# High and low halves in tiles of their own, the shared tap first and on head 1, and a new spread of first loads, weight conversion and softmax products

## The chip, the cores and the metric

The kernel runs on one core of a Trainium2 chip. The metric is the device time of one execution in microseconds, the median of the runs. The core's engines work side by side, each through its own list in order: PE (the matrix engine, its weight loads shown as PEld), DVE (the vector engine), ACT (the scalar engine), POOL, and SP, which issues DMAs. Engines wait for one another through semaphores.

## The reference

```
qn = q / (norm(q, axis=1) + 1e-6);  kn = k / (norm(k, axis=1) + 1e-6)      # B=4, N=6336, C=256
s = kn^T @ qn / tau                     # 256 x 256 per batch: attention between channels
a = softmax(s);  x = v @ a              # the attention's output
g = sum over k of conv_w[k] * x[t-4+k]  # causal convolution along N, five taps per channel
out = (sigmoid(g) * (x @ w_val)) @ w_out
```

q, k, v and the output are float32, 4 x 6336 x 256. The weights come as 64-bit floats; the kernel takes them as pairs of 32-bit words and turns them into float32 on the chip.

## The kernel before, in words

**Row groups.** For each batch b, q and k are read in 17 groups of three row tiles (128 rows each); group 0 has one full tile and one of 64 rows. `group_tasks` loads a group into `raw`; ACT squares it (`sq`), and DVE or POOL adds the squares into running sums (`acc_ps` on DVE, `acc` on POOL). PE multiplies k by q into the batch's 256 x 256 sum in PSUM (`s_ps`, L481). A tile is multiplied either whole in fp32 (operands `raw`) or split: ACT casts it to a high half (L413), POOL subtracts to get the low half (L416), and PE multiplies high by high, low by high and high by low. High and low lie in one tile, `hi`. Of batch 0, the first groups are whole and then two tiles of three.

**Softmax.** Once all groups of a batch are in, a chain of small tasks `("M", b, ...)` makes the attention matrix. DVE joins the sums of squares (acc, L518); PE sums over rows (norms, L514); ACT takes the root (L525); DVE inverts (L529 to L534); ACT makes a diagonal (L539); PE spreads it (L546); DVE scales (L550); ACT takes the exponentials (L556) and divides (L568); PE transposes (L581) and multiplies by `w_val` (combine, L591). High and low halves of both results (L572, L575 on POOL; high_w L595 on ACT, low_w L598 on DVE) are what the steps multiply by.

**Steps.** 52 steps n, 13 a batch, cover 508 rows each (240 the last of a batch). A step loads v, transposes it (DVE, L659), casts it high (ACT, L663) and low (POOL, L666). For each head h, a half of the 256 channels, PE makes x (X, `x_ps`, L674), ACT multiplies by tap 0 into `gate` (G, L697) and DVE adds the other taps (D, L700). ACT takes the sigmoid (Z, L711), PE makes the values (U, `val_ps`), DVE multiplies (B, L718), ACT and POOL make high and low halves (H, L724; J, L727), and PE makes the output (F, L746), which ACT copies (L755) and SP stores. In the late steps (36 to 50), which have no row groups beside them, the last tap of one head is shared: ACT makes it in a tile of its own, `part` (G+, L705), and POOL adds it (D+, L708).

**Weights.** `prepare_weights` (L309 to L337) is a generator of DVE operations on 32-bit words, one task each. `w_ps` is its scratch in PSUM, `w_raw` the words in SBUF; val and out are 128 x 512, the convolution's weight is 128 x 10.

**What sets the order.** Nothing is ordered by hand but PE's list, `line`, built at the end: all groups of batch 0, then steps with groups of later batches between them, and the four softmax products of a batch dropped in one at a time by `chain`. The class `Plan` holds tasks with costs, dependencies and buffers, works out due times from `line`, and picks for each engine in turn; `emit` fixes that order in the program. Costs of tasks are numbers in the source. `WANTED` gives due times in us for the weights' tasks.

Of the kernel before, what the change touches and what calls it, by code (L numbers as in the profile page):

```python
# [17 lines left out]
P = 128  # L18
GROUP = 3
# [8 lines left out]
class Plan:  # L28
# [65 lines left out]
    def run(self, line):  # L94
# [21 lines left out]
        dma_free, lanes = 0.0, []  # L116
# [18 lines left out]
        while len(order) < len(T):  # L135
# [76 lines left out]
def kernel(  # L212
# [70 lines left out]
    w_raw = {}  # L283
# [22 lines left out]
    def prepare_weights(part):  # L306
# [6 lines left out]
        if WORDS == 2:  # L313
# [15 lines left out]
            nc.vector.tensor_scalar(up, up, 0xFFE00, 3, ALU.bitwise_and, ALU.logical_shift_left)  # L329
            yield  # L330
            nc.vector.tensor_tensor(up, up, f, ALU.bitwise_or)
# [10 lines left out]
    PREP = {"val": 10, "conv": 10, "out": 9}  # L342

    def weight_tasks():
# [5 lines left out]
        for part in ("val", "conv", "out"):  # L350
            gen = {}
            n = PREP[part] if WORDS == 2 else 1
            for k in range(n):
# [4 lines left out]
                if part != "conv" and k == 6:  # L358
                    cost = 1.25
# [4 lines left out]
                  "out": lambda: WORDS == 2 and nc.scalar.copy(wo_hi.rearrange("p h e -> p (h e)"), w_raw["out"][:, :, 1].bitcast(F32))}[part],  # L364
                 deps=[("prep", part, n - 1)], uses=[holds[part]])
# [7 lines left out]
    def group_tasks(b, g):  # L373
# [14 lines left out]
        def load():  # L388
            raw = t["raw4"] = raw_p.tile([P, 2, GROUP, C], F32, name="raw")
            for s, src in ((0, q), (1, k)):  # L390
                eng = nc.scalar if b == 0 and g < 2 and s else nc.sync
                main = src[b, 0:RP * P].rearrange("(p j) c -> p j c", j=RP)
                eng.dma_start(out=raw[:, s, 0:n, :], in_=main[:, j0_:j0_ + n, :])
                if g == 0 and REST:
                    eng.dma_start(out=raw[0:REST, s, n, :], in_=src[b, RP * P:N])
            if (b, g) == (0, 1):
# [3 lines left out]
        issues = (4 if g == 0 and REST else 2) // (2 if b == 0 and g < 2 else 1)  # L400
# [6 lines left out]
        for u, (np_, ja, jb) in enumerate(split):  # L407
            r, js = slice(0, np_), slice(ja, jb)

            def cast(r=r, js=js, u=u):  # L410
                if u == 0:
                    t["hi"] = split_p.tile([P, GROUP, 2, 2, C], F32R, name="hi")
                nc.scalar.copy(t["hi"][r, js, :, 0, :], t["raw"][r, js, :, :])  # L413

            def low(r=r, js=js):
                nc.gpsimd.tensor_tensor(t["hi"][r, js, :, 1, :], t["raw"][r, js, :, :], t["hi"][r, js, :, 0, :].bitcast(F32), ALU.subtract)  # L416
# [35 lines left out]
        for u, part in enumerate(squares):  # L452
# [3 lines left out]
            for j in range(ja, jb):  # L456
                task(("A", b, g, j), dict(DVE=0.6, POOL=1.25), None, lambda engine, np_=np_, j=j: add(np_, j, engine),
# [14 lines left out]
        def mms(np_, j, whole=True, halves=((0, 0), (0, 1), (1, 0))):  # L472
            r = slice(0, np_)
            stop = g == NG - 1 and (np_, j) == rows[-1] and (whole or len(halves) > 1)
            for h in range(NH):
                if whole:
                    ops = [(dealt(t["raw"][r, j, 1, :], h), t["raw"][r, j, 0, :])]
                else:
                    ops = [(dealt(t["hi"][r, j, 1, x, :], h), t["hi"][r, j, 0, y, :]) for x, y in halves]
                for n_, (lhs, rhs) in enumerate(ops):  # L480
                    nc.tensor.matmul(st["s"][:, h, :], lhs, rhs, start=False, stop=stop and h == NH - 1 and n_ == len(ops) - 1)  # L481
            if (b, g) == (0, 0) and j == n:
# [21 lines left out]
    def softmax_tasks(b):  # L504
# [410 lines left out]
```

## Time and profile before

| | us |
|---|---|
| median of 3 runs | 604.43 (603.49 to 607.92) |
| profiled execution, its own time | 606.84 |
| its span in the profile | 605.0 (1.84 lie outside) |
| granted TensorE clock | 1.0 |

Each row of a group gives line, engine, operation, tiles and the count, then busy us and mean ns. Rows in order of time begin with the start in us and the time taken; a bracket gives idle time ahead of it and what ended that. The span starts at 0; batch 0's products end near 51 us, the batches' steps begin near 65, 214, 359 and 504.

### The profile page before, as it was taken

The page shows a single profiled execution, that of the slowest core. Times are in us where ns is not written, and L with a number is a line of the kernel's source. Part 1 is how long each engine was busy: PE and PEld are TensorE (multiplying, and loading weights), DVE is VectorE, ACT ScalarE, POOL GpSimd, SP SyncE. Part 2 cuts the span into 40 slices and gives each one's busy share as a digit, 9 for nine tenths or more (in the row PEclk, how much of TensorE's full clock was granted, in tenths as well). Part 3 has the DMA queues.
Part 4 walks back from the last instruction along what each step waited for, and adds up shares of the span by engine and source line. Part 5 has one row for each costly group of instructions (what it writes and reads, how often), then busy time and mean ns, then how long its engine had stood idle before and what let it go on. Part 6 is the DMA issues. An engine that isn't in the chain of part 4 may idle for free.

```text
span 605.0 us, 10549 instructions
## 1 busy us (share of the span) xinstructions
PE 594.2 (98%) x3659; PEld 533.2 (88%) x3659; DVE 510.2 (84%) x789; ACT 474.3 (78%) x588; POOL 504.1 (83%) x241
## 2 busy tenths in 40 slices
PE   8999999999999999999999999999999999999996
PEld 6988898999989988998998988998988998888886
DVE  2997799999877999969777899978977979888774
ACT  5768999789889979689689978878677876677645
POOL 3977999999979999989986999988973777577653
PEclk9999999999999999999999999999999999999999
DMA  8999958696674968889465888769646353554213
GB/s 297 387 364 282 232 126 200 170 192 141 194 192 126 224 151 219 167 201 204 126 175 140 218 203 198 162 148 233 143 122 132 79 143 91 131 138 112 59 57 121
DMA packets 154944, 105.84 MB, mean 175 GB/s; under 512 B 111114, under 2 KB 137994, under 8 KB 154890
## 3 DMA queue, kind: packets, MB, share of 16 engines
q1 hardware_dynamic: 154387, 104.45, 68.5%
q10 hardware_dynamic: 503, 0.71, 0.4%
q8 instruction: 29, 0.48, 0.3%
q14 instruction: 25, 0.20, 0.1%
HBM read 79.18 MB, written 25.95 MB: 174 GB/s over the span
## 4 chain that ended last, share of the span: by engine, by line
PE 52%; DVE 24%; POOL 7%; issue 6%; ACT 6%; DMA 4%; SPq 1%; POOLq 0%; DVEq 0%; ACTq 0%
PE s_ps L481 13%; PE x_ps L674 13%; DVE gate L700 12%; PE o_ps L746 12%; PE val_ps L674 12%; DVE acc_ps L444 6%; POOL g_lo L727 3%; DVE gate L718 3%; DMA v_raw<-in_v_dram 2%; DMA raw<-in_k_dram 2%; POOL gate L708 1%; DVE v_raw L659 1%; POOL hi L416 1%; ACT g_hi L724 1%; PE o_ps L591 1%
## 5 line engine op out<-in xcount | busy, mean ns | idle before, releaser
L700 DVE SCALAR_TENSOR_TENSOR gate<-x_ps,wa,gate 128x508 f32<-128x508 f32 (+1 forms) x401 | 272.5, 717 | 28.3 <-POOL g_lo L727 9.1
L416 POOL TENSOR_TENSOR hi<-raw,hi 128x1536 fp32r<-128x1536 f32 (+2 forms) x65 | 182.5, 2811 | 16.8 <-ACT hi L413 11.5
L727 POOL TENSOR_TENSOR g_lo<-gate,g_hi 128x1016 fp32r<-128x1016 f32 (+2 forms) x52 | 120.2, 2312 | 20.7 <-ACT g_hi L724 20.7
L444 DVE TENSOR_TENSOR acc_ps<-acc_ps,sq 128x512 f32<-128x512 f32 (+1 forms) x145 | 100.5, 693 | 42.9 <-ACT sq L440 39.2
L666 POOL TENSOR_TENSOR v_lo<-v_raw,v_hi 128x1024 fp32r<-128x1024 f32 (+1 forms) x52 | 123.4, 2373 | 6.6 <-ACT v_hi L663 5.2
L481 PE MATMUL s_ps<-hi 128*128 128x256 f32 x918 | 126.5, 288 | 1.3 <-POOL hi L416 1.3
L481 PEld LDWEIGHTS s_ps<-hi 128*128 128x128 f32 x918 | 117.9, 196 | 4.8 <-POOL hi L416 2.7
L674 PE MATMUL x_ps<-v_hi,w 128*128 128x512 f32 (+2 forms) x416 | 110.3, 385 | 1.5 <-DVE gate L700 1.5
L674 PE MATMUL val_ps<-v_hi,w 128*128 128x508 f32 (+1 forms) x416 | 107.7, 380 | 0.0
L440 ACT ACTIVATE sq<-raw 128x1536 f32<-128x1536 f32 (+2 forms) x68 | 95.9, 1413 | 7.3 <-DVE acc_ps L444 5.3
L674 PEld LDWEIGHTS val_ps<-v_hi,w 128*128 128x128 f32 x416 | 75.9, 188 | 14.9 <-DVE gate L718 0.2
L413 ACT CAST hi<-raw 128x1536 fp32r<-128x1536 f32 (+2 forms) x65 | 77.8, 1200 | 13.1 <-DMA raw<-in_k_dram 13.1
L724 ACT CAST g_hi<-gate 128x1016 fp32r<-128x1016 f32 (+3 forms) x54 | 52.8, 978 | 44.6 <-DVE gate L718 44.3
L674 PEld LDWEIGHTS x_ps<-v_hi,w 128*128 128x128 f32 x416 | 72.7, 188 | 14.6 <-issue 2.3
L746 PE MATMUL o_ps<-wo_hi,g_hi 128*127 128x256 f32 (+1 forms) x396 | 79.2, 281 | 0.0
L746 PE MATMUL o_ps<-wo_lo,g_hi 128*127 128x256 f32 (+1 forms) x396 | 79.0, 281 | 0.0
L755 ACT COPY o_sb<-o_ps 127x512 f32<-127x512 f32 (+1 forms) x99 | 57.5, 589 | 27.4 <-PE o_ps L746 27.2
L444 POOL TENSOR_TENSOR acc<-acc,sq 128x512 f32<-128x512 f32 (+1 forms) x47 | 61.1, 1301 | 14.4 <-ACT sq L440 12.7
L718 DVE TENSOR_TENSOR gate<-val_ps,gate 128x508 f32<-128x508 f32 (+1 forms) x104 | 67.0, 656 | 4.3 <-ACT gate L711 4.3
L697 ACT ACTIVATE gate<-x_ps,wa 128x508 f32<-128x508 f32 (+1 forms) x104 | 68.2, 662 | 1.2 <-PE x_ps L674 1.1
L711 ACT ACTIVATE gate<-gate 128x1016 f32<-128x1016 f32 (+1 forms) x52 | 53.2, 1024 | 18.5 <-DVE gate L700 18.5
L746 PE MATMUL o_ps<-wo_hi,g_lo 128*127 128x256 f32 (+1 forms) x396 | 64.0, 284 | 1.9 <-POOL g_lo L727 1.9
(84 smaller groups left out, 740.7 us busy)
## 6 DMA issues: line engine op xcount, KB each, us to landing
raw<-in_q_dram SPq DMA_DIRECT2D x64, 384.0 KB, 6.2
v_raw<-in_v_dram SPq DMA_DIRECT2D x192, 128.0 KB, 6.0
raw<-in_k_dram SPq DMA_DIRECT2D x63, 384.0 KB, 6.8
out_dram<-o_sb SPq DMA_DIRECT2D x47, 448.0 KB, 3.2
out_dram<-o_sb SPq DMA_DIRECT2D x47, 60.0 KB, 3.0
v_raw<-in_v_dram SPq DMA_DIRECT2D x16, 64.0 KB, 2.1
out_dram<-o_sb SPq DMA_DIRECT2D x3, 240.0 KB, 2.6
raw<-in_q_dram SPq DMA_DIRECT2D x4, 128.0 KB, 3.1
```

Of the source, the lines that this page charges most:

```text
L413: nc.scalar.copy(t["hi"][r, js, :, 0, :], t["raw"][r, js, :, :])
L416: nc.gpsimd.tensor_tensor(t["hi"][r, js, :, 1, :], t["raw"][r, js, :, :], t["hi"][r, js, :, 0, :].bitcast(F32), ALU.subtract)
L440: nc.scalar.activation(t["sq"][0:np_, ja:jb], t["raw"][0:np_, ja:jb], AF.Square)
L444: eng.tensor_tensor(st[key][0:np_], st[key][0:np_], t["sq"][0:np_, j], ALU.add)
L481: nc.tensor.matmul(st["s"][:, h, :], lhs, rhs, start=False, stop=stop and h == NH - 1 and n_ == len(ops) - 1)
L666: nc.gpsimd.tensor_tensor(t["vl"][:, :, 0:g, :], t["v"], t["vh"][:, :, 0:g, :].bitcast(F32), ALU.subtract)
L674: nc.tensor.matmul(dst, weights[b][:, which, ws, ch, hs], vs[:, ch, at + lo:at + hi_], start=n_ == 0, stop=n_ == len(ops) - 1)
L697: nc.scalar.activation(t["gate"][:, h, 0:w], t["x", h][:, 0:w], AF.Copy, scale=cw[:, h, 0:1])
L700: nc.vector.scalar_tensor_tensor(t["gate"][:, h, 0:w], t["x", h][:, k_:k_ + w], cw[:, h, k_:k_ + 1], t["gate"][:, h, 0:w], ALU.mult, ALU.add)
L718: nc.vector.tensor_tensor(t["gate"][:, h, 0:w], t["val", h][:, 0:w], t["gate"][:, h, 0:w], ALU.mult)
L727: eng.tensor_tensor(t["gl"][:, hs, 0:w], t["gate"][:, hs, 0:w], t["gh"][:, hs, 0:w].bitcast(F32), ALU.subtract)
L746: nc.tensor.matmul(t["o", p][0:rows, u * C:(u + 1) * C], gs[:, h, j * rows:(j + 1) * rows], ws[:, h, :], start=(u, n_) == (0, 0) if HEADS ...
```

## The change

1. The split tile `hi` becomes two tiles, `hi` (both operands' high halves) and `lo`. The products are the same.
2. In steps 36 to 50 the shared last tap is that of head 1 instead of head 0, and POOL adds it before DVE's taps of that head instead of after head 0's.
3. First loads: q's 64 rows go to ACT's queue and group 1's k to SP's. The 64-row tile's products follow group 2's. Only group 0's first tile has extra zero products behind it.
4. Loads of `w_val` and `w_out` move ahead of group 6's, those of the convolution's weight behind them.
5. In the weight conversion two operations that wrote to `w_raw` become three that write to PSUM.
6. The softmax products of batches 1 to 3 are spread by `SPREAD`: each of the last three skips one call of `chain`.
7. Costs in the planner change, and it counts table loads of ACT.

```diff
-START, HOP, DRAIN, SLOT, FLIGHT, REACH, RATE = 4.8, 0.12, 0.4, 0.45, 4.5, 1.6, 340000.0
+START, HOP, DRAIN, SLOT, FLIGHT, REACH, RATE = 4.8, 0.12, 0.22, 0.45, 4.5, 1.6, 340000.0
...
-WANTED = {("load", "conv"): 16, ("load", "val"): 17, ("load", "out"): 24, ("ready", "val"): 40, ("ready", "out"): 48}
+SPREAD = (0, 1, 1, 1)
+TABLE = 1.28
+WANTED = {("load", "conv"): 30, ("load", "val"): 17, ("load", "out"): 26, ("ready", "val"): 40, ("ready", "out"): 48}
...
-            nc.vector.tensor_scalar(up, up, 0xFFE00, 3, ALU.bitwise_and, ALU.logical_shift_left)
+            low = wo_lo.rearrange("p h e -> p (h e)") if part == "out" else w
+            nc.vector.scalar_tensor_tensor(low, lo, 2.0 ** -35, fs, ALU.mult, ALU.mult)
             yield
-            nc.vector.tensor_tensor(up, up, f, ALU.bitwise_or)
+            nc.vector.tensor_scalar(f, f, 3, None, ALU.logical_shift_right)
             yield
-            dst = wo_lo.rearrange("p h e -> p (h e)") if part == "out" else fs
-            nc.vector.scalar_tensor_tensor(dst, lo, 2.0 ** -35, fs, ALU.mult, ALU.mult)
+            nc.vector.scalar_tensor_tensor(f, up, 0xFFE00, f, ALU.bitwise_and, ALU.bitwise_or)
+            yield
+            nc.vector.tensor_scalar(f, f, 3, None, ALU.logical_shift_left)
+            w_high[part] = fs
             if part != "out":
                 yield
-                nc.vector.tensor_tensor(w, fs, up.bitcast(F32), ALU.add)
+                nc.vector.tensor_tensor(w, w, fs, ALU.add)
...
-                eng = nc.scalar if b == 0 and g < 2 and s else nc.sync
+                eng = nc.scalar if b == g == 0 and s else nc.sync
...
-                    eng.dma_start(out=raw[0:REST, s, n, :], in_=src[b, RP * P:N])
+                    (nc.scalar if b == 0 else nc.sync).dma_start(out=raw[0:REST, s, n, :], in_=src[b, RP * P:N])
...
-                    t["hi"] = split_p.tile([P, GROUP, 2, 2, C], F32R, name="hi")
-                nc.scalar.copy(t["hi"][r, js, :, 0, :], t["raw"][r, js, :, :])
+                    t["hi"], t["lo"] = [split_p.tile([P, GROUP, 2, C], F32R, name=name) for name in ("hi", "lo")]
+                nc.scalar.copy(t["hi"][r, js], t["raw"][r, js, :, :])
...
-            few = K - 1 if shared and h == 0 else K
+            few = K - 1 if shared and h == 1 else K
+            if few < K:
+                part_i = ("sq", "part", n)
+                task(("G+", n), "ACT", 0.06 + 0.51 * part, lambda h=h: last_tap(h), deps=[("G", n, h)], uses=[x_i, part_i], takes=[part_i])
+                task(("D+", n), "POOL", 0.1 + 1.15 * part, lambda h=h: add_tap(h), deps=[("G+", n)], uses=[part_i, gate_i])
...
-            if few < K:
-                part_i = ("sq", "part", n)
-                task(("G+", n), "ACT", 0.06 + 0.51 * part, lambda h=h: last_tap(h), deps=[("X", n, h)], uses=[x_i, part_i], takes=[part_i])
-                task(("D+", n), "POOL", 0.1 + 1.15 * part, lambda h=h: add_tap(h), deps=[("G+", n), ("D", n, h, few - 1)], uses=[part_i, gate_i])
...
+        if (b, g) == (0, 0):
+            kept.extend(rows[2:])
+            rows = rows[:2]
         line.extend(rows)
+        if (b, g) == (0, 2):
+            line.extend(kept)
         if g == NG - 1:
-            pending.extend(mm(b, "norms", "spread", "transpose", "combine"))
+            names = mm(b, "norms", "spread", "transpose", "combine")
+            for key, wait in zip(names, SPREAD if b else (0,) * 4):
+                pending.extend([None] * wait + [key])
```

Lines of the changed program lie six or so further down. The first place is SP's queue at the start; the 128x256 rows are group 0's full tile, 64x256 its rest, 128x768 a later group. Before:

```order
L393 DMA raw_106<-in_q_dram 128x256
L395 DMA raw_106<-in_q_dram 64x256
L393 DMA raw_111<-in_q_dram 128x768
L393 DMA raw_115<-in_q_dram 128x768
L393 DMA raw_115<-in_k_dram 128x768
```

Now, up to the loads of the two big weights:

```order
L399 DMA raw_106<-in_q_dram 128x256
L399 DMA raw_112<-in_q_dram 128x768
L399 DMA raw_112<-in_k_dram 128x768
L399 DMA raw_115<-in_q_dram 128x768
...
L399 DMA raw_132<-in_q_dram 128x768
L399 DMA raw_132<-in_k_dram 128x768
L308 DMA w_raw_137<-in_moe_w_val_dram 128x2x512
L308 DMA w_raw_152<-in_moe_w_out_dram 128x2x512
L399 DMA raw_175<-in_q_dram 128x768
```

The 64 rows of q left this queue, group 1's k (`raw_112`) came into it, and both weights stand ahead of group 6 (`raw_175`).

The second place is DVE around the end of batch 0's sums of squares (acc_all) up to the invert of the norms. Before:

```order
L331 TENSOR_TENSOR w_raw_230<-w_raw_230,w_ps_353 128x512
L334 SCALAR_TENSOR_TENSOR wo_lo_100<-w_raw_230,w_ps_353 128x512
L444 TENSOR_TENSOR acc_ps_126<-acc_ps_126,sq_461 128x512 x2
L444 TENSOR_TENSOR acc_ps_126<-acc_ps_126,sq_471 128x512 x2
L518 TENSOR_TENSOR acc_all_502<-acc_ps_126,acc_137 128x512
L529 TENSOR_SCALAR o_ps_506<-o_ps_506 128x4
```

Now:

```order
L450 TENSOR_TENSOR acc_ps_128<-acc_ps_128,sq_476 128x512 x2
L326 TENSOR_SCALAR w_ps_424<-w_raw_273 128x10
L328 TENSOR_SCALAR w_ps_424<-w_ps_424 128x10
L524 TENSOR_TENSOR acc_all_508<-acc_ps_128,acc_135 128x512
L330 TENSOR_SCALAR w_ps_424<-w_ps_424 128x10
L332 SCALAR_TENSOR_TENSOR w_ps_424<-w_raw_273,w_ps_424 128x10
...
L345 TENSOR_TENSOR wa_97<-wa_97,w_ps_424 128x10
L369 RECIPROCAL rtau_95<-tau_sb_96 128x1
L665 STREAM_TRANSPOSE v_raw_388<-v_raw_388 128x2x512
L535 TENSOR_SCALAR o_ps_519<-o_ps_519 128x4
```

Two conversions of the convolution's weight stand ahead of the sum, seven more, the reciprocal and the first step's transpose between the sum and the invert.

The third place is ACT in a late step, from its sigmoid (L711, now L717) to the next step's output copies. Before:

```order
L711 ACTIVATE gate_5715<-gate_5715 128x1016
L697 ACTIVATE gate_5803<-x_ps_5784,wa_97 128x508
L705 ACTIVATE part_5805<-x_ps_5784,wa_97 128x508
L697 ACTIVATE gate_5803<-x_ps_5796,wa_97 128x508
```

Now:

```order
L717 ACTIVATE gate_5781<-gate_5781 128x1016
L703 ACTIVATE gate_5870<-x_ps_5850,wa_97 128x508
L703 ACTIVATE gate_5870<-x_ps_5863,wa_97 128x508
L711 ACTIVATE part_5882<-x_ps_5863,wa_97 128x508
```

The part (L705, now L711) went from the place behind head 0's gate to behind head 1's. On POOL, in the same steps, before:

```order
L708 TENSOR_TENSOR gate_5803<-gate_5803,part_5805 128x508
L727 TENSOR_TENSOR g_lo_5869<-gate_5715,g_hi_5868 128x1016
L666 TENSOR_TENSOR v_lo_5848<-v_raw_5648,v_hi_5847 128x1024
L708 TENSOR_TENSOR gate_5892<-gate_5892,part_5894 128x508
```

Now:

```order
L714 TENSOR_TENSOR gate_5870<-gate_5870,part_5882 128x508
L672 TENSOR_TENSOR v_lo_5914<-v_raw_5714,v_hi_5913 128x1024
L733 TENSOR_TENSOR g_lo_5936<-gate_5781,g_hi_5935 128x1016
L714 TENSOR_TENSOR gate_5959<-gate_5959,part_5971 128x508
```

The low half of a later step's v now comes ahead of the gate's low half, right behind the shared tap's add. On DVE, the first of a step's taps no longer waits for the part, and head 1's first tap waits for POOL's add.

More of the change, by code (lines that the diff above doesn't have):

```diff
@@ L33, in __init__, with task @@
         self.tasks = {}
-    def task(self, key, engine, cost, emit, deps=(), uses=(), takes=(), lead=()):
+    def task(self, key, engine, cost, emit, deps=(), uses=(), takes=(), lead=(), table=None):
         assert key not in self.tasks, key
-        self.tasks[key] = dict(key=key, engine=engine, cost=cost, emit=emit, deps=list(deps), lead=dict(lead), uses=list(dict.fromkeys(list(uses) + list(takes))),
+        self.tasks[key] = dict(key=key, engine=engine, cost=cost, emit=emit, deps=list(deps), lead=dict(lead), table=table, uses=list(dict.fromkeys(list(uses) + list(takes))),
                                takes=list(takes), order=len(self.tasks))
@@ L115, in run @@
                 opened(key)
-        dma_free, lanes = 0.0, []
+        dma_free, lanes, table = 0.0, [], None
         order = []
@@ L168, in run @@
                 free[e] = start + self.duration(t, e)
+                if t["table"] and t["table"] != table:
+                    table = t["table"]
+                    free[e] += TABLE
                 end = free[e] + (DRAIN if e == "PE" else HOP if e else 0)
@@ L282 @@
     parts_w = {"val": wa[:, 0:NW], "conv": wa[:, NW:], "out": wb}
-    w_raw = {}
+    w_raw, w_high = {}, {}
     def load_weights(*names):
@@ L357, in weight_tasks @@
                 cost = 0.6 if part != "conv" else 0.1
-                if part != "conv" and k == 6:
-                    cost = 1.25
                 task(("prep", part, k), "DVE", cost, emit, deps=[("load", part) if k == 0 else ("prep", part, k - 1)],
@@ L363, in weight_tasks @@
                  {"val": lambda: None, "conv": lambda: nc.vector.reciprocal(rtau, tau_sb),
-                  "out": lambda: WORDS == 2 and nc.scalar.copy(wo_hi.rearrange("p h e -> p (h e)"), w_raw["out"][:, :, 1].bitcast(F32))}[part],
-                 deps=[("prep", part, n - 1)], uses=[holds[part]])
+                  "out": lambda: WORDS == 2 and nc.scalar.copy(wo_hi.rearrange("p h e -> p (h e)"), w_high["out"])}[part],
+                 deps=[("prep", part, n - 1)], uses=[holds[part], ("bank", "w", part)])
     def dealt(row, h):
@@ L456, in group_tasks @@
             for j in range(ja, jb):
-                task(("A", b, g, j), dict(DVE=0.6, POOL=1.25), None, lambda engine, np_=np_, j=j: add(np_, j, engine),
+                task(("A", b, g, j), dict(DVE=0.7, POOL=1.25), None, lambda engine, np_=np_, j=j: add(np_, j, engine),
                      deps=[("S", b, g, u)] + [("B", b, x) for x in accs], uses=[sq_i] + list(accs.values()))
@@ L478, in mms @@
                 else:
-                    ops = [(dealt(t["hi"][r, j, 1, x, :], h), t["hi"][r, j, 0, y, :]) for x, y in halves]
+                    ops = [(dealt(t[("hi", "lo")[x]][r, j, 1, :], h), t[("hi", "lo")[y]][r, j, 0, :]) for x, y in halves]
                 for n_, (lhs, rhs) in enumerate(ops):
                     nc.tensor.matmul(st["s"][:, h, :], lhs, rhs, start=False, stop=stop and h == NH - 1 and n_ == len(ops) - 1)
-            if (b, g) == (0, 0) and j == n:
+            if (b, g, j) == (0, 0, 0):
                 idle(2)
@@ L837 @@
     todo = [(bg, rows_of[bg]) for bg in all_groups]
-    pending = []
+    pending, kept = [], []
     def take_group():
@@ L850, in chain @@
             if pending:
-                line.append(pending.pop(0))
+                key = pending.pop(0)
+                if key:
+                    line.append(key)
     for _ in range(NG):
@@ L870 @@
             if all_steps[n + 1][0] != all_steps[n][0]:
-                chain(4)
+                chain(len(pending))
             line += [("X", n + 1, h) for h in range(NH)]
```

29 lines of the change are left out of this document (15 added, 14 removed).

## The prediction

> **What bounds the kernel now.** I read the page's share of busy time first, then the chain that ended last, then what PE, the matrix engine, waited for (us in total, times, longest).
>
> ```profile
> PE 594.2 (98%) x3659; PEld 533.2 (88%) x3659; DVE 510.2 (84%) x789; ACT 474.3 (78%) x588; POOL 504.1 (83%) x241
> PE 52%; DVE 24%; POOL 7%; issue 6%; ACT 6%; DMA 4%; SPq 1%; POOLq 0%; DVEq 0%; ACTq 0%
> ...
> PE o_ps L746 <- POOL g_lo L727: 1.9, 3, 0.9
> PE x_ps L674 <- DVE gate L700: 1.5, 2, 0.8
> PE s_ps L481 <- POOL hi L416: 1.3, 3, 0.6
> ```
>
> PE is busy for 98% of 605.0 us, and every product is kept. So the change can win only PE's pauses, its slow first stretch and the small gaps between matmuls. The orders elsewhere change too (square sums dealt anew between DVE and POOL), where PE is full. The second line warns that 24% of the chain is DVE: in places PE is paced by another engine. The other three rows give the pauses: POOL's low halves at the end (1.9 us), vector taps (1.5), POOL's low halves in batch 0 (1.3).
>
> ```profile
> 30.00:45.00 15.00, 14.07 (x80) 12.36 (x79) 14.73 (x23) 9.66 (x10) 10.88 (x9) 1.00 1.01 365
> 180.00:195.00 15.00, 15.00 (x104) 13.96 (x104) 9.81 (x15) 14.99 (x19) 12.43 (x6) 1.00 0.48 141
> 570.00:585.00 15.00, 14.16 (x79) 12.16 (x78) 10.09 (x16) 9.49 (x14) 11.02 (x6) 1.00 0.23 71
> ```
>
> The table by stage has window, then busy us of PE, PEld, DVE, ACT, POOL. In 180 to 195 PE is full, in 30 to 45 and 570 to 585 about 0.9 us is open. The steady middle offers nothing; four places do, and I price each.
>
> **Start.** Two groups of products, from 3.6 to 7.6 and from 11 to 16 us, and three rows in order of time:
>
> ```profile
> L481 PE MATMUL s_ps<-raw 128*128 128x256 f32 (+1 forms) x8 | 4.1, 673 | 0.0
> L481 PE MATMUL s_ps<-raw 128*128 128x256 f32 x25 | 5.6, 379 | 0.0
> ...
> 5.70 1.35 PEld L481 LDWEIGHTS s_ps<-raw 64*128 64x128 f32 x4 [0.65 <-DMA raw<-in_q_dram]
> 8.72 7.95 PE L481 MATMUL s_ps<-raw 128*128 128x256 f32 x32
> 1.18 0.54 ACTq L395 DMA_DIRECT2D raw<-in_k_dram  x1
> ```
>
> Early products take 673 ns instead of 379, and the 64-row tile's run in that slow stretch. The change puts its four products behind group 2 and lets group 1's two loads follow q0 directly. Four of eight took half of 4.1 us; four of the 32 that follow take an eighth of 7.95, 1.0. So PE could be 1.05 earlier, and 0.65 more if the pause for that tile goes; k0 now stands behind one more issue on ACT's queue, 0.54. That is 0 to 1.7 for PE alone. It doesn't count by itself: the norms of batch 0 wait for the sum of squares on DVE, priced next. It counts as cover for PE's other waits up to there.
>
> **Sum of squares in batch 0.** DVE is 14.73 of 15 us busy; its work ahead of the sum sets it.
>
> ```profile
> 27.74 3.19 DVE L329 TENSOR_SCALAR w_raw<-w_raw 128x512 int32<-128x512 int32 x1
> L329 DVE TENSOR_SCALAR w_raw<-w_raw 128x512 int32<-128x512 int32 x2 | 3.6, 1809 | 0.0
> 20.05 0.69 DVE L329 TENSOR_SCALAR w_raw<-w_raw 128x10 int32<-128x10 int32 x1
> L331 DVE TENSOR_TENSOR w_raw<-w_raw,w_ps 128x512 int32<-128x512 int32 x2 | 1.4, 678 | 0.0
> L323 DVE TENSOR_SCALAR w_ps<-w_ps 128x512 int32<-128x512 int32 x2 | 1.4, 700 | 0.0
> 51.03 0.69 DVE L518 TENSOR_TENSOR acc_all<-acc_ps,acc 128x512 f32<-128x512 f32 x1
> 51.78 1.08 PE L514 MATMUL o_ps<-ones,acc_all 128*128 128x1 f32 x8 [0.24 <-DVE acc_all L518]
> ```
>
> Two big weights lose L329 (3.6 us together) and L331 (1.4), 5.0, and gain three operations each in forms of L323 (0.70), 4.2: 0.8 less. The convolution weight's ten operations (nine near 0.17, as the small L529 of the next fence but one, and the 0.69) and the reciprocal come to 2.4; only two of its new ones, 0.3, still stand ahead of the sum: 2.0 less. Together 2.8. Bounds: 0.3 if the long operation's stall (3.19 - 0.69) only moves to a neighbour, 3.1 if loads that start earlier add 0.3. I take 2.5, near the full count, as the new forms read or write PSUM as L323 does, and its two take 0.70 each. So the norms start at 49.3 instead of 51.78. [...]
>
> PE must keep up. Its waits for POOL before that (1.3) shrink, since the two high-high products of a tile no longer stand behind POOL; at 7.95/32 = 0.25 each the pair covers 0.5 us of each wait, and the longest is 0.6. With the earlier start that is enough.
>
> The two big weights now load ahead of group 6, both at once.
>
> ```profile
> 15.00:30.00 15.00, 15.00 (x86) 13.95 (x85) 14.03 (x28) 11.49 (x12) 15.00 (x13) 1.00 1.02 386
> ```
>
> The transfers are full there (share 1.02). At 386 GB/s the 1.05 MB take 2.7 us; the convolution's loads that stood there before leave, so group 6 lands some 2.2 us later, and ACT's squares with it. DVE then has conversions to do, so I price that at nothing; without that cover up to 2.2 us of the 2.5 are gone.
>
> **Chain of batch 0.** What was moved off comes back here.
>
> ```profile
> 53.08 0.17 DVE L529 TENSOR_SCALAR o_ps<-o_ps 128x4 f32<-128x4 f32 x1 [1.36 <-ACT o_ps L525]
> ...
> 57.32 1.24 DVE L659 STREAM_TRANSPOSE v_raw<-v_raw 128x1024 f32<-128x1024 f32 x1
> ...
> 63.75 1.59 PEld L591 LDWEIGHTS o_ps<-wa,at 128*128 128x128 f32 x8 [0.39 <-ACT at L585]
> ```
>
> Between the sum and the invert (L529) now stand seven conversions and the reciprocal, 0.17 each, and the first transpose, 1.24: 2.6 us in a hole of 1.36, so the chain is 1.2 us later behind its sum; at best nothing, as the transpose no longer stands at 57.32, ahead of the exponentials' total. PE has next-batch products to fill, as before, but paused 0.39 before the combine already. Step 0's low_w moves behind its eight taps, but its value products move behind step 1's gate products, which cover it. I give back 1.1, a little less (0 to 1.7, with 0.6 for that if the cover is short). The stage nets 2.5 - 1.1 = **1.4** (-1.4 to 2.5).
>
> **First steps of batches 1 and 2.**
>
> ```profile
> 207.67 2.94 DVE L444 TENSOR_TENSOR acc_ps<-acc_ps,sq 128x512 f32<-128x512 f32 x4
> 210.52 5.83 DVE L700 SCALAR_TENSOR_TENSOR gate<-x_ps,wa,gate 128x508 f32<-128x508 f32 x8
> 215.06 1.15 PE L674 MATMUL x_ps<-v_hi,w 128*128 128x512 f32 x4 [0.77 <-DVE gate L700]
> ```
>
> PE waits 0.77 us for a tap that started late, behind four sums of squares; the waits at both places are 1.5 by the second table. Between the last short taps and these stand five sums now instead of seven, 2 x 0.73 = 1.5 us less, so the waits can go. Bounds 0 and 0.95 each, with the small gaps around; the chain's later pieces land in the same stretch, so I take 0.65 each, **1.3**. Smaller waits of this sort at other places: 0.2 (-0.5 to 0.5).
>
> **Late steps with the shared tap.**
>
> ```profile
> 515.48 0.40 PE L746 MATMUL o_ps<-wo_hi,g_hi 128*127 128x256 f32 x2
> 523.79 0.40 PE L746 MATMUL o_ps<-wo_hi,g_hi 128*127 128x256 f32 x2
> 565.76 0.40 PE L746 MATMUL o_ps<-wo_hi,g_hi 128*127 128x256 f32 x2
> 574.24 0.40 PE L746 MATMUL o_ps<-wo_hi,g_hi 128*127 128x256 f32 x2
> 573.10 1.05 ACT L711 ACTIVATE gate<-gate 128x1016 f32<-128x1016 f32 x1
> 574.06 0.67 ACT L697 ACTIVATE gate<-x_ps,wa 128x508 f32<-128x508 f32 x1
> 574.63 0.68 ACT L705 ACTIVATE part<-x_ps,wa 128x508 f32<-128x508 f32 x1
> 575.39 2.18 DVE L700 SCALAR_TENSOR_TENSOR gate<-x_ps,wa,gate 128x508 f32<-128x508 f32 x3 [2.39 <-ACT part L705]
> 581.61 1.05 ACT L711 ACTIVATE gate<-gate 128x1016 f32<-128x1016 f32 x1
> 571.15 1.28 POOL L708 TENSOR_TENSOR gate<-gate,part 128x508 f32<-128x508 f32 x1 [2.01 <-DVE gate L700]
> 584.64 0.74 PE L746 MATMUL o_ps<-wo_hi,g_lo 128*127 128x256 f32 x4 [0.84 <-POOL g_lo L727]
> ```
>
> A step takes PE 8.31 us at 515, 8.48 at 565. From one sigmoid (L711) to the next is 8.51 us: ACT's sigmoid, gate and shared part, then DVE's taps, which start on the part (the row at 575.39 says so). That loop is longer than PE's 8.31, so a lag builds, paid from 565 on in steps of 8.48 and at 584.64 in a wait for POOL's low half. After the change the first tap waits for the first gate alone, 574.63 - 574.06 = 0.57 earlier: the loop is 7.9, under 8.31, and PE sets the pace. Gain: 1.9 of waits, some four steps of 0.17 and about 0.2 of small gaps around each of the three waits, 3.2; bounds 0.7, if only the stretching goes and the ends stay, and 3.5. I take **3.2**. The added wait is DVE's on POOL: head 1's taps wait for POOL's add (1.28). On ACT the part now comes third, so it ends about 1.1 us after the first tap starts and the add 1.3 later; ahead of head 1's first tap stand four taps at 0.73 and two products of the step before, near 0.7 each (as a tap): 4.3. Slack 1.9 if POOL is free. Behind a waiting tap stand the step's other taps, B and the sigmoid.
>
> **The sum.** 1.4 + 1.3 + 0.2 + 3.2 = 6.1; 0.7 off for waits that new orders bring and no row shows: 5.4. Span 605.0 - 5.4 = 599.6; the profiled execution, 606.84 with 1.84 around its span, becomes 601.4. That execution lay 2.4 above the median 604.43, so the median becomes **599.0**.
>
> **Rivals.** (1) *All terms in full*: 2.5 + 1.9 + 0.5 + 3.5 = 8.4, 596.0. For it: the waits are all named in rows; against: they'd have to vanish with no new one. (2) *Front gains eaten*: batch 0's chain takes all of it and the first steps keep their waits, 3.2 remains less 0.7: 602. For it, the late group 6 and the 0.39 pause ahead of the combine; against, DVE's shorter list is plain. (3) *The change doesn't loosen the late loop*: POOL is inside an operation of its own (it has the low halves of v and of the gate) when the part comes. If the part waits 0.5 us longer than the slack of 1.9, the loop is 8.4, as good as before: only front and first steps remain, 2.9 less 0.7: 602.2. (4) *Slower*, one mechanism: the softmax products of batches 1 to 3 come some 10 us later, and DVE's low_w stands in line for them ahead of step 12's taps, where DVE is full.
>
> ```profile
> 178.64 1.99 PE L591 MATMUL o_ps<-wa,at 128*128 128x256 f32 x8
> ...
> 190.51 0.68 DVE L598 TENSOR_TENSOR w<-o_ps,w 128x512 fp32r<-128x512 f32 x1
> ```
>
> Now low_w found its operand waiting, as PE's combine was done at 180.6, ten us before. Moved by ten, that room is gone. Each us that DVE then stands there is one us of PE at the next batch's first steps, three times. From 2.3 us of standing it eats the whole gain; at 3.5 it costs 10.5 less what the lighter stretch takes up (0.5 each time): 599.0 + 9 = 608.
>
> **How the numbers follow.** Forecast 0.55, rival 1 0.18, rivals 2 and 3 0.20 together, rival 4 0.07. About 1%, 6 us, is what a measurement of this kernel can tell from no change, so faster means below 598.4: rival 1 and two fifths of the forecast, 0.41; slower needs 610.5, the far part of rival 4, 0.04. Range: rivals 1 to 3 with the bounds of the terms, 595.5 to 604.0.
>
> **What would show it.** Right: norms near 49.3, no operation over 1 us among the conversions, the vector taps at 215 and 360 without PE waits, steps 8.3 us apart up to the end, no wait of 0.8 on POOL's low half. Wrong: PE waiting around the combine of batch 0 for over 1.5 us, DVE waiting at low_w near 197, or head 1's taps waiting for POOL's add.

## The result, and the profile after

The changed kernel takes **601.28 us** (median of 15 runs, 600.33 to 602.59), the kernel before 604.58 in the same comparison (15 runs, 603.49 to 607.92): ratio 0.9934, 95% interval 0.9917 to 0.9951. It is 3.3 us faster, 0.5%; the forecast was 5.4 us, and 599.0, with a range of 595.5 to 604.0. The profiled execution of after took 600.84 with a span of 598.7. Its span is 6.3 us under the one of before, more than the medians differ by, since the profiled execution of before lay 2.3 above the median of its kernel and this one 0.4 below; the last 0.3 lie outside the span.

The page's share of busy time and the chain, after:

```profile
PE 589.5 (98%) x3659; PEld 533.0 (89%) x3659; DVE 506.4 (85%) x790; ACT 478.3 (80%) x588; POOL 506.7 (85%) x243
PE 95%; DVE 2%; ACT 1%; DMA 1%; issue 0%; ACTq 0%; DVEq 0%
```

PE's part of the chain went from 52% to 95%: nearly everywhere PE now sets the pace. What it waited for:

```profile
PE s_ps L487 <- DMA raw<-in_k_dram: 3.3, 1, 3.3
PE s_ps L469 <- DVE zeros L273: 1.6, 1, 1.6
PE x_ps L680 <- DVE gate L706: 0.4, 1, 0.4
PE o_ps L597 <- ACT at L591: 0.2, 1, 0.2
```

The waits for POOL's low halves are gone, and so are both for DVE's taps at 215 and 360; the 0.4 that is listed is a new one, at 71 us. Another new one stands on top: 3.3 us for a load of k. Busy time by stretch (PE, PEld, DVE, ACT, POOL), the first row before, the others after:

```profile
0.00:15.00 15.00, 13.38 (x39) 9.70 (x40) 4.14 (x7) 8.39 (x11) 4.98 (x10) 1.00 0.87 296
...
0.00:15.00 15.00, 10.09 (x33) 8.09 (x34) 4.45 (x8) 8.74 (x11) 5.32 (x10) 1.00 0.89 317
30.00:45.00 15.00, 15.00 (x87) 14.00 (x86) 14.83 (x26) 13.29 (x13) 14.80 (x13) 1.00 1.00 304
205.00:220.00 15.00, 15.00 (x96) 13.58 (x95) 14.58 (x23) 13.26 (x16) 15.00 (x7) 1.00 0.94 223
570.00:585.00 15.00, 15.00 (x94) 13.46 (x93) 10.64 (x16) 8.46 (x13) 7.07 (x5) 1.00 0.17 52
```

PE is full in three of the four stretches that the prediction priced, and has lost more than before in the first. The start, in order of time, with the load and the first product of before ahead of the first dots, and how long that load took to land (KB, us):

```profile
0.73 0.41 ACTq L393 DMA_DIRECT2D raw<-in_k_dram  x1
3.70 4.08 PE L481 MATMUL s_ps<-raw 128*128 128x256 f32 x8
raw<-in_k_dram ACTq DMA_DIRECT2D x1, 128.0 KB, 2.9
...
1.33 0.60 ACTq L399 DMA_DIRECT2D raw<-in_k_dram  x1
6.99 2.05 PE L487 MATMUL s_ps<-raw 128*128 128x256 f32 x4 [3.31 <-DMA raw<-in_k_dram]
9.68 8.83 PE L487 MATMUL s_ps<-raw 128*128 128x256 f32 x36
20.25 0.62 ACT L419 CAST hi<-raw 128x512 fp32r<-128x512 f32 x1 [2.44 <-DMA raw<-in_k_dram]
46.94 0.68 DVE L524 TENSOR_TENSOR acc_all<-acc_ps,acc 128x512 f32<-128x512 f32 x1
51.02 0.97 PE L520 MATMUL o_ps<-ones,acc_all 128*128 128x1 f32 x8
```

k's first tile was issued at 1.33 instead of 0.73, took 5.5 us instead of 2.9 to land, and the first product starts at 6.99 instead of 3.70. ACT's wait of 2.44 us at 20.25 is for group 6, which is late as the prediction said. DVE's sum of squares comes 4.1 us earlier (46.94, it was 51.03), but the norms only 0.8, as PE's products now end last.

To see where the 6.3 us of span came from I summed, by stretch, how far matmuls started beyond their usual distance in the two traces:

| stretch, us | before | after | forecast gain | gain |
|---|---|---|---|---|
| 0 to 30 | 3.1 | 4.9 | | -1.8 |
| 30 to 75 | 3.0 | 0.9 | | 2.1 |
| **front together** | 6.1 | 5.8 | 1.4 | **0.3** |
| first steps of batches 1 and 2 (210 to 225, 345 to 375) | 2.3 | 0.1 | 1.3 | **2.2** |
| 420 to 435, 465 to 480 | 0.8 | 0.7 | 0.2 | 0.1 |
| late steps (540 to 600) | 3.6 | 0.1 | 3.2 | **3.5** |

The rows add up to 6.1. What follows the last product is 0.5 us shorter, and small gaps elsewhere give 0.3 back: 6.3. The late steps, in order of time:

```profile
563.01 0.40 PE L752 MATMUL o_ps<-wo_hi,g_hi 128*127 128x256 f32 x2
566.52 1.07 ACT L717 ACTIVATE gate<-gate 128x1016 f32<-128x1016 f32 x1
568.21 2.31 DVE L706 SCALAR_TENSOR_TENSOR gate<-x_ps,wa,gate 128x508 f32<-128x508 f32 x3 [1.94 <-ACT gate L703]
570.20 1.29 POOL L714 TENSOR_TENSOR gate<-gate,part 128x508 f32<-128x508 f32 x1 [1.41 <-ACT part L711]
571.02 0.74 DVE L706 SCALAR_TENSOR_TENSOR gate<-x_ps,wa,gate 128x508 f32<-128x508 f32 x1
571.32 0.40 PE L752 MATMUL o_ps<-wo_hi,g_hi 128*127 128x256 f32 x2
574.84 1.07 ACT L717 ACTIVATE gate<-gate 128x1016 f32<-128x1016 f32 x1
```

Steps are 8.31 us apart at 563 and sigmoids 8.32: PE's pace. DVE waits 1.94 for the gate alone, and POOL's add, 570.20 to 571.49, is done before DVE reaches head 1's taps, at 572.27.

### The profile page after: what moved, and what is told of

Same layout as the page of the kernel before. It is cut to its first block, busy times and chain, and to the rows that moved or that the text cites. A ratio compares the mean times of both kernels' runs of the same rounds, so it can differ in the third digit from the quotient of the medians.

```text
span 598.7 us, 10539 instructions
## 1 busy us (share of the span) xinstructions
PE 589.5 (98%) x3659; PEld 533.0 (89%) x3659; DVE 506.4 (85%) x790; ACT 478.3 (80%) x588; POOL 506.7 (85%) x243
## 4 chain that ended last, share of the span: by engine, by line
PE 95%; DVE 2%; ACT 1%; DMA 1%; issue 0%; ACTq 0%; DVEq 0%
PE s_ps L487 25%; PE o_ps L752 23%; PE x_ps L680 22%; PE val_ps L680 22%; DVE gate L706 1%; DMA raw<-in_k_dram 1%; PE o_ps L597 1%; PE o_ps L520 1%; PE o_ps L552 0%; PE x_ps L752 0%; ACT gate L703 0%; PE o_ps L587 0%; ACT L717 0%; ACT gate L717 0%; DVE s L556 0%
## 5 line engine op out<-in xcount | busy, mean ns | idle before, releaser
L422 POOL TENSOR_TENSOR lo<-raw,hi 128x1536 fp32r<-128x1536 f32 (+2 forms) x65 | 182.6, 2816 | 19.9 <-ACT hi L419 18.2
L672 POOL TENSOR_TENSOR v_lo<-v_raw,v_hi 128x1024 fp32r<-128x1024 f32 (+1 forms) x52 | 123.8, 2380 | 13.2 <-ACT v_hi L669 13.0
L450 DVE TENSOR_TENSOR acc_ps<-acc_ps,sq 128x512 f32<-128x512 f32 (+1 forms) x143 | 99.0, 693 | 33.5 <-ACT sq L446 30.2
L487 PE MATMUL s_ps<-lo,hi 128*128 128x256 f32 x306 | 76.9, 285 | 0.0
L487 PE MATMUL s_ps<-hi,lo 128*128 128x256 f32 x306 | 76.2, 283 | 0.0
L450 POOL TENSOR_TENSOR acc<-acc,sq 128x512 f32<-128x512 f32 x49 | 63.7, 1300 | 10.7 <-ACT sq L446 9.7
L669 ACT CAST v_hi<-v_raw 128x1024 fp32r<-128x1024 f32 (+1 forms) x52 | 57.6, 1108 | 14.8 <-PE val_ps L680 13.2
L752 PEld LDWEIGHTS o_ps<-wo_hi,g_hi 128*127 128x127 f32 (+1 forms) x396 | 62.9, 187 | 3.5 <-ACT o_sb L761 0.3
L665 DVE STREAM_TRANSPOSE v_raw<-v_raw 128x1024 f32<-128x1024 f32 (+1 forms) x52 | 62.1, 1196 | 3.2 <-DMA v_raw<-in_v_dram 3.2
```

The source lines that it names most:

```text
L422: nc.gpsimd.tensor_tensor(t["lo"][r, js], t["raw"][r, js, :, :], t["hi"][r, js].bitcast(F32), ALU.subtract)
L450: eng.tensor_tensor(st[key][0:np_], st[key][0:np_], t["sq"][0:np_, j], ALU.add)
L672: nc.gpsimd.tensor_tensor(t["vl"][:, :, 0:g, :], t["v"], t["vh"][:, :, 0:g, :].bitcast(F32), ALU.subtract)
L752: nc.tensor.matmul(t["o", p][0:rows, u * C:(u + 1) * C], gs[:, h, j * rows:(j + 1) * rows], ws[:, h, :], start=(u, n_) == (0, 0) if HEADS ...
```

## The experiments

They were measured in several rounds. The kernel before took 604.58 to 604.92 beside them, so times of different rounds can be compared to some 0.3 us. Dots in a piece of code stand for lines left out.

**The kernel before once more.** 

> The kernel before, unchanged, profiled once more. The 15 times of before fall in two heaps, 603.5 to 604.6 (nine) and 606.3 to 607.9 (six), and the profiled execution of before (606.84) lies in the upper one; those of after make one heap, 600.3 to 602.6. Theory A: the heaps of before differ at one place, so that a second profile in the lower heap has a span near 602 and one stretch that is 2.5 to 3 us shorter (the start, where PE's matmuls go at half pace up to 10.4 us, is my first guess). Theory B: the profiled execution was only late by small bits everywhere: a new span of 602 to 605 with the same gaps, each a little smaller.

It took 609.09, span 607.3. That is the upper heap again, so neither theory was tried as meant; but its start (matmuls 0.43 us apart instead of 0.22, PE's half pace, until 14.1 us; 10.5 in the first profile) and one DVE operation differ. The wide L329 in order of time, in this run, in the first experiment below and in the last:

```profile
28.33 4.47 DVE L329 TENSOR_SCALAR w_raw<-w_raw 128x512 int32<-128x512 int32 x1
...
27.32 1.13 DVE L329 TENSOR_SCALAR w_raw<-w_raw 128x512 int32<-128x512 int32 x1
...
27.97 4.47 DVE L329 TENSOR_SCALAR w_raw<-w_raw 128x512 int32<-128x512 int32 x1
```

The operation that I priced at 3.19 takes 1.13 to 4.47 from run to run. DVE's sum moves with it: it begins at 48.56, 51.03, 52.53 and 52.87 where the operation took 1.13, 3.19, 4.47 and 4.47.

**The shared tap alone.**

```diff
-            few = K - 1 if shared and h == 0 else K
+            few = K - 1 if shared and h == 1 else K
...
+                task(("D+", n), "POOL", 0.1 + 1.15 * part, lambda h=h: add_tap(h), deps=[("G+", n)], uses=[part_i, gate_i])
...
```

> Before, with the shared tap alone changed (head 1, first). Theory A, that the shared tap's place made the late lag: PE's waits for POOL's low half after 550 us vanish and steps stay 8.31 us apart to the end, 3.4 us off the span, time 600.9 to 601.7. Rival: the late waits went because of the planner's new costs or because the late stage begins earlier; then this kernel is within 0.7 of before, 603.9 to 604.6.

603.63 (602.25 to 606.23, 12 runs; before 604.78 beside it), ratio 0.998, interval 0.9961 to 0.9999. PE's waits in its profile:

```profile
PE x_ps L674 <- DVE gate L700: 2.0, 4, 0.8
...
PE x_ps L674 <- ACT v_hi L663: 0.7, 1, 0.7
PE x_ps L674 <- POOL v_lo L666: 0.6, 1, 0.6
...
PE o_ps L746 <- POOL g_lo L727: 0.2, 1, 0.2
```

The late waits went (1.9 to 0.2; the gaps from 540 on from 3.6 to 0.1 us), so theory A's mechanism is shown. Its time is not, and the measured one lies between theory A's and the rival's: the planner dealt the first late steps anew, and near 467 to 471 PE now waits for DVE, ACT and POOL, 2.7 us more than before.

**k's first tile first.**

```diff
-                if g == 0 and REST:
-                    (nc.scalar if b == 0 else nc.sync).dma_start(out=raw[0:REST, s, n, :], in_=src[b, RP * P:N])
+                if g == 0 and REST and b:
+                    nc.sync.dma_start(out=raw[0:REST, s, n, :], in_=src[b, RP * P:N])
+            if b == g == 0 and REST:
+                for s, src in ((0, q), (1, k)):
+                    nc.scalar.dma_start(out=raw[0:REST, s, n, :], in_=src[b, RP * P:N])
```

> After, with one edit: on ACT's queue k's first tile is issued ahead of the 64 rows of q instead of behind them. Theory A, that the first product waited 3.3 us because k's first tile lost its place among the first three transfers: it lands near 3.8 instead of 6.85, the first product starts there instead of at 6.99, and as half of this time is spent at half pace up to about 10.5 us, PE is 1.5 to 2.0 us earlier at the norms of batch 0 (51.0 now), time 599.3 to 599.9. Rival 1: the start is hidden behind DVE's sum of squares: 601.0 to 601.5. Rival 2: the half pace ends earlier too, by as much as the first product is earlier: 3 us, 598.2.

598.30 (597.35 to 598.61, 6 runs), ratio to before 0.9882, interval 0.9855 to 0.991: 3.0 us faster than the changed kernel, by a change of two DMAs' places. Every other instruction stands where it stood. It is the fastest version here.

```profile
0.74 0.42 ACTq L399 DMA_DIRECT2D raw<-in_k_dram  x1
3.78 2.08 PE L490 MATMUL s_ps<-raw 128*128 128x256 f32 x4
6.96 2.35 PE L490 MATMUL s_ps<-raw 128*128 128x256 f32 x8 [0.24 <-DMA raw<-in_k_dram]
45.93 0.68 DVE L527 TENSOR_TENSOR acc_all<-acc_ps,acc 128x512 f32<-128x512 f32 x1
48.26 0.97 PE L523 MATMUL o_ps<-ones,acc_all 128*128 128x1 f32 x8
```

The first product is back at 3.78 and the norms come at 48.26, 2.8 earlier. I had expected 1.5 to 2, half of it lost to the half pace; rival 2 had the size right, for matmuls started 0.22 us apart from 7.8 us on (after: from 10.8).

**Zeros in the wait.**

`idle(n)` issues n products of zeros.

```diff
-                idle(3)
+                idle(11)
```

> After (601.3), with eight more products of zeros at the start, in the 3.5 us in which PE waits for k's first tile; the loads and all orders stay. Theory A, that PE's half pace ends when PE has been busy for some 3.5 us without a pause: it ends near 7 us instead of 10.7, group 1 runs at full pace, PE reaches the norms 1.5 to 2 us earlier: 599.2 to 600.0. Rival 1: the end of the half pace is a matter of when and not of what PE did: 601.0 to 601.6. Rival 2: products of zeros hold k's first product up, or zeros do not count as work: 601.0 to 602.

599.23 (598.89 to 599.93, 6 runs), 2.05 faster than the changed kernel, with the loads where they were. Theory A's time holds, and the half pace ends sooner than it said, at 5.2 instead of near 7.

```profile
2.18 4.06 PE L476 MATMUL s_ps<-zeros 128*128 128x512 f32 x11
6.70 1.11 PE L487 MATMUL s_ps<-raw 128*128 128x256 f32 x4 [0.46 <-DMA raw<-in_k_dram]
8.11 1.67 PE L487 MATMUL s_ps<-raw 128*128 128x256 f32 x7
```

Zeros started 0.43 us apart up to 5.17 and 0.23 from there on; four real products take 1.11 us here and 2.05 after. From the first zeros at 1.59 to the end of the half pace are 3.6 us, near theory A's 3.5. So the late load cost the change twice: PE stood still for 3.31 us, and its half pace lasted until 10.7 instead of 5.2.

**Zeros and k first.** On the kernel with k first, `idle(3)` becomes `idle(4)`, and `idle(2)` behind the first tile becomes `idle(4)` too. 

> The kernel with k's first tile first (598.3), with three more products of zeros, one ahead of the first product and two in the pause ahead of group 1. Theory A: its half pace ended at 7.8 us; with no pause it ends near 6.9 and the times lie closer together: 597.4 to 598.1. Rival: nothing left to gain there, 598.2 to 598.8.

598.56 (597.98 to 598.89, 6 runs): the rival, nothing more to gain. The half pace ended near 5.1 in its profile, and then PE waited 1.35 us for the next load of k.

**The 64-row tile back at the start.**

```diff
+            if (b, g) == (0, 0):
+                if j == 1:
+                    return
+                for n_, j_ in rows:
...
+                return idle(2)
```

The first task of group 0 now multiplies both its tiles, the second nothing.

> The kernel with k's first tile first (598.3), with the 64-row tile's four products back behind tile 0's, as before the change; every other instruction and all orders stay. Theory A, that the tile's place decides when PE's half pace ends: PE must wait for the tile's loads (7.1 us in that kernel), works at half pace until about 10.5 instead of 7.8 us, and loses about 2.5 to 3 us: 600.8 to 601.3. Rival 1: the half pace ends near 7.8 all the same and only the pause for the loads and the tile's slow products cost: 1.0 to 1.5 us, 599.3 to 599.8. Rival 2: hidden behind DVE's sum of squares: 598.3.

601.95 (597.98 to 602.57, 12 runs), 3.65 slower than with k first: theory A's direction and 0.7 more than its size. The profiled run was the one of twelve at 597.98. There PE waited for the tile and was at full pace all the same:

```profile
7.09 1.11 PE L487 MATMUL s_ps<-raw 64*128 64x256 f32 x4 [1.38 <-DMA raw<-in_k_dram]
```

Eleven others took 599.95 to 602.57. That the half pace lasted longer in them is the likely reading, but no trace of them shows it, so this experiment leaves the tile's place unpriced.

**High and low in one tile again**, on the kernel with k first, the orders kept.

```diff
-                nc.gpsimd.tensor_tensor(t["lo"][r, js], t["raw"][r, js, :, :], t["hi"][r, js].bitcast(F32), ALU.subtract)
+                nc.gpsimd.tensor_tensor(t["hi"][r, js, :, 1, :], t["raw"][r, js, :, :], t["hi"][r, js, :, 0, :].bitcast(F32), ALU.subtract)
...
```

> The kernel with k's first tile first (598.3), with high and low halves again in one tile; the orders stay. Theory A: POOL's low half is late by 0.3 to 0.6 us for some tiles of batch 0, where PE now sets the pace; the two high-high products no longer cover it: PE waits for POOL come back, 0.3 to 1.0 us, 598.6 to 599.3. Rival: POOL is far enough ahead once DVE's long operation is gone, and nothing changes: 598.0 to 598.6.

603.47 (601.92 to 604.25, 12 runs), 5.2 slower: the largest difference of all, and neither theory had it.

```profile
67.35 6.89 POOL L425 TENSOR_TENSOR hi<-raw,hi 128x1536 fp32r<-128x1536 f32 x2 [0.20 <-DMA raw<-in_k_dram]
70.86 1.22 PE L490 MATMUL s_ps<-hi 128*128 128x256 f32 x4 [3.65 <-POOL hi L425]
```

PE stands 3.65 us before high-high products of batch 1 until the first of two POOL operations (6.89/2 = 3.4 each) is done. In the kernel with k first the same wait isn't there: the high-high products start at 67.17, while POOL's operations run from 67.49 on. Then PE's products of the next step take longer (window 70.8 to 74.5, against 76 to 80, where PE is at full pace):

```profile
L683 PE MATMUL x_ps<-v_hi,w 128*128 128x512 f32 x5 | 2.3, 581 | 0.0
...
L683 PE MATMUL val_ps<-v_hi,w 128*128 128x508 f32 x8 | 2.2, 391 | 0.0
```

**The split alone**, the same edit the other way round on the kernel before. 

> Before, with high and low halves in tiles of their own and nothing else; the orders stay those of before. Theory A, that the split is worth something only where the planner's order puts POOL's low half late, as in the changed kernel: here PE's waits for POOL (1.3 us in the profile of before) came with DVE's long operation and stand ahead of a sum that DVE ends, so nothing is won: within 0.7 of before's median, 603.9 to 605.3. Rival: the waits for POOL are PE's own loss: 1.0 to 1.8 us faster, 602.9 to 603.7.

605.83 (603.13 to 608.45, 12 runs; before 604.92), ratio 1.0004, interval 0.998 to 1.0028: nothing, as theory A says. The split is worth 5.2 us in the new order, which puts high-high products ahead of POOL's low half, and nothing in the old. In batch 0 it isn't what took the waits for POOL away: alone it leaves 1.0 us of them (1.0 and 1.3 in the two profiles of before), and without it the new order has none there.

**The conversion alone.** The edit is that of the change, with its task counts. 

> Before, with the weight conversion's operations alone changed. Theory A: no operation of the conversion takes over 1 us (the one of 3.19 us is gone), DVE's sum of squares of batch 0 comes 1 to 3 us earlier than 51.03, but PE's products of batch 0 end at 51.5 anyway, so the norms gain 0.3 to 0.5 only: 604.0 to 604.5. Rival: PE's end there is itself set by DVE (through ACT's squares, which waited 1.9 us for DVE's adds): norms 2.5 us earlier, 602.1.

606.32 (605.67 to 608.07, 12 runs; before 604.78), ratio 1.0023, interval 1.0006 to 1.004: slower than either. The norms came at 49.5, as the rival says, but the planner dealt the middle anew, and PE waits 2.1 us for POOL near 129 and 1.5 for DVE near 215. So the next experiment keeps the old order.

**The conversion in the old order.**

```diff
-            nc.vector.tensor_scalar(up, up, 0xFFE00, 3, ALU.bitwise_and, ALU.logical_shift_left)
-            yield
-            nc.vector.tensor_tensor(up, up, f, ALU.bitwise_or)
...
+            nc.vector.scalar_tensor_tensor(low, lo, 2.0 ** -35, fs, ALU.mult, ALU.mult)
+            nc.vector.tensor_scalar(f, f, 3, None, ALU.logical_shift_right)
+            yield
+            nc.vector.scalar_tensor_tensor(f, up, 0xFFE00, f, ALU.bitwise_and, ALU.bitwise_or)
...
```

> Before, with the new operations of the weight conversion emitted from the old tasks, so that every engine's order is that of before, with one short DVE operation more per weight. In three profiles of the old conversion the first wide L329 took 1.13, 3.19 and 4.47 us. Theory A, that this collision with POOL's work makes the upper heap of times: no operation of the conversion is over 1 us, the upper heap (606 to 608) is gone, all times 602.5 to 605, median 603.3 to 604.2, 0.5 to 1.5 under before's. Rival: the heaps come from the start (when the first loads land and when the half pace ends), and stay: highest over 606, median within 0.4 of before's.

605.37 (603.91 to 608.74, 12 runs; before 604.58), ratio 1.0022, interval 0.9998 to 1.0046. No operation of the conversion takes over 1 us, and still four runs of twelve are above 607.7. Theory A falls. The profile is of such a run (608.74), and in it the start, the rival's cause, isn't it either: the half pace ended at 10.9, and at 10.7 in the run of the shared tap with 603.43. From 52.5 to 56.3 us, right behind a wait of 1.26 us for the sum and the norms' products of one column:

```profile
L483 PE MATMUL s_ps<-raw 128*128 128x256 f32 (+1 forms) x8 | 3.9, 650 | 0.0
```

PE is at half pace. The four upper runs have a granted clock of 0.993 to 0.995, the eight others 0.999 to 1.0. So here the upper heap is most likely this stretch at half pace; one profile and the clocks speak for it. In the two profiles of before it was not: those products took 2.1 us for eight there, and L329 3.19 and 4.47. In the two profiles with 4.47 the half pace of the start also lasted longer (13.5 and 14.1 us, against 10.5 and 10.7 where L329 took 3.19 and 1.13), so what divides before's own heaps stays open.

**No spread**, on the kernel with k first; the planner deals some things anew.

```diff
-SPREAD = (0, 1, 1, 1)
+SPREAD = (0, 0, 0, 0)
```

> The kernel with k's first tile first (598.3), with SPREAD all zeros; the planner then orders some things anew. Theory A, that DVE's lighter list and not the spread took the waits at the first steps of batches 1 and 2 away: no PE wait over 0.3 us near 210 and 355, time 598.0 to 598.9. Rival: the spread did it, the waits of about 0.8 come back at both places, 599.5 to 600.5.

599.99 (599.43 to 601.73, 6 runs), 1.7 slower. Windows of its profile:

```profile
205.00:220.00 15.00, 14.07 (x88) 12.44 (x87) 13.86 (x21) 12.73 (x16) 14.10 (x8) 1.00 0.95 222
350.00:365.00 15.00, 15.00 (x96) 13.53 (x95) 14.62 (x22) 11.89 (x15) 13.37 (x7) 1.00 1.00 217
```

PE has lost 0.9 us again near 215, and nothing near 355: half to the rival, half to theory A. This profiled run is the slowest of the six (601.73). It has a wait of 2.1 us for k's second load at the start, ahead of all that the edit moved, and half pace behind it from 8.3 to 11.6; so the 1.7 us of the medians are not accounted for place by place.

**The weights' due times back**, on the kernel with k first: `WANTED` as before the change. 

> The kernel with k's first tile first (598.3), with the due times of the weights' loads and conversions as before the change; the planner then orders some things anew. Theory A, that the place of these loads is worth nothing since PE, not DVE, sets the pace to the norms (DVE's sum is done 2.3 us before): within 0.6 of 598.3, group 6 lands about 1.5 us earlier, and no PE wait over 0.5 us in the first 75 us. Rival: the loads' place is what made DVE's sum early; then the norms are later by 1 to 2 us: 599.3 to 600.3.

603.23 (601.78 to 605.4, 12 runs), 4.9 slower, and not for either theory's reason. The loads' place wasn't undone: both big weights were still issued ahead of group 6, at 11.1, 12.1 and 13.2 us, and ACT still waited 2.85 us for it. And the norms came at 50.1 because PE was at half pace until 11.2, though the first loads and products stand in the order of the kernel with k first (7.8). What cost most stands far from the weights:

```profile
PE o_ps L755 <- POOL g_lo L736: 1.6, 2, 1.3
...
PE x_ps L683 <- DVE gate L709: 1.3, 1, 1.3
```

The longest lie near 359 and 420: two due times of the first 30 us changed what the planner did there. What the loads' place is worth stays open.

## Why the prediction was right or wrong

**Start: the step of the mechanism that failed.** "k0 now stands behind one more issue on ACT's queue, 0.54" counted the issue, not the transfer. Behind 64 rows of q and beside group 1's q the tile landed at 6.85 instead of 3.65, 3.2 us late. The 0.65 that I counted for the 64-row tile's pause was idle time of PEld, the weight loads; PE's own row showed none there. I also said the start doesn't count by itself; that held while DVE's sum set the norms, and stopped holding when the sum came 4.1 us earlier. Putting k first gave 3.0 us back: with it the norms are at 48.26, where I had put them at 49.3, and the time 598.3, where I had 599.0.

**Sum of squares: right in sign, too small, and hardly paid.** 4.1 us instead of 2.5 in these two executions, of which the norms kept 0.8. And 2.5 of the price was one operation's stall in one execution, which took 1.13 us in another; without it, in the old order, the kernel is no faster (1.0022). In the trace of before the wide L329 took 0.42 us where POOL stood idle as it began (45.10) and 3.19 where POOL had one operation behind the other (27.74); in the three other profiles of the old conversion the wide L329 near 28 us took 1.13 and twice 4.47. The wide operations of the new conversion took 0.68 to 0.70 in the trace of after, all beside operations of POOL: L323's 0.70, which I had put in for them, and no stall. That POOL's work is what held L329 up is my estimate from these rows; no experiment tried it alone. The profiles also show how much the stall varies between executions, which one could not.

**From the profile to the median: the step that cost the number.** The profiled execution was forecast at 601.4 and took 600.84. From there I took off 2.4, as before's profiled execution lay that far above its median; after's lies 0.4 under its own. Together that is 2.8 us, more than the whole miss from 599.0 to 601.28, and it is why the profiled times fell by 6.0 and the medians by 3.3. I took prices from an execution above its median and gave them to the median. That L329 is what lay above it is likely and not shown. The sum itself came near by luck in part: by the table the front fell 1.1 short, first and late steps gave 1.2 more, and the 0.7 held back for new waits was not needed beside them.

**PE keeping up: hidden in the wrong place.** I let the split cover waits of 0.6 us in batch 0. What it covers is a wait of 3.65 at batch 1's first high-high products (5.2 us with what follows), because the new order relies on it. In the old order it is worth nothing, and batch 0's own waits went without it.

**Chain of batch 0.** I gave back 1.1, for conversions between the sum and the invert. They cost nothing: as PE's products ended last, DVE still stood idle for 2.33 us ahead of the invert (52.41), and from the norms to the combine it took 11.9 us, 12.0 before. What came instead lies behind the chain: the stretch from 60 to 75 us lost 0.6 more than before (0.7 to 1.3), 0.43 of it at 71 in a wait for DVE's taps.

**First steps: right, undersized.** 2.2 instead of 1.3. Without the spread one of the two places comes back, so the spread holds that one; that DVE's lighter list holds the other is argued, not shown.

**Late steps: right.** 3.5 against 3.2. The loop starts on the first gate, POOL's add is on time, PE's pace holds to the end; the tap alone takes the same waits away.

**Rivals.** The first half of rival 2, the front eaten, happened, by another mechanism than the two that I named; its second half, that the first steps keep their waits, did not. That its 602 lies nearer to 601.28 than my 599.0 is chance. Rival 3 did not: POOL stood idle for 1.41 us when the part came (570.20). Rival 4 did not: the profile shows no idle time of DVE ahead of any low_w, and the stretch of 205 to 220 is full.

## What to carry to other kernels

Price the first transfers by when they land, not by when they are issued, and count what PE's standing still costs twice, once in time and once in pace (here 3.31 us of wait, and a half pace until 10.7 instead of 5.2). Before a wait from one profile is priced, look whether the profiled execution lies at its kernel's median; a stall of one operation may be there in some executions alone (L329: 1.13 to 4.47 us in four). Under a planner, undoing one part deals all the others anew: an experiment that keeps every order tells what the part is worth, one that doesn't tells what the new deal is worth.

## What the runs showed of the hardware

At the start matmuls of 256 columns stood 0.43 us apart instead of 0.22, PE's half pace. It did not end at a fixed time. With zeros one after another from 1.59 us on it ended at 5.2, 3.6 us later; in the changed kernel at 10.7, 3.7 us behind the first product after the wait of 3.31; in the kernel before, whose first products started up to 0.66 and 0.83 us apart, at 10.5 in one execution and at 14.1 in another, though PE was at work there from 1.59 on as well. So the runs show no one length of work that ends it.

Behind waits of 1.26, 2.1 and 3.65 us (the conversion in the old order, no spread, one tile) products ran at half pace, and the granted clock of these executions was 0.993, 0.996 and 0.997. Behind waits of 1.38 and 1.35 at the start of two other runs (the 64-row tile back; zeros and k first) they did not, with a clock of 1.0.

The granted clock of the windows' table reads 1.00 for the first 15 us of the changed kernel, though its first products ran at half pace, 0.43 us apart; only the distance of the matmuls shows it. Behind the waits of 2.1 and 1.26 us the clock does show it: 0.89 for the first 15 us without the spread, 0.57 from 51 to 57 us in the profile of the conversion in the old order.
